# Where the top half of a float64 weight is merged: a second ScalarE pass into PSUM and one shift-or, for 36 of 64 tiles

## The chip, the cores and the metric

One Trainium2 chip, one core of it. The metric is device time of one execution in microseconds, as a median over several runs.

## The reference, cut to what matters

A block-wise linear attention (2 batches, 8 heads, 768 tokens, head size 64), a layer with a two-dimensional Fourier mix and a residual MLP (512 to 2048 to 512), and a second residual MLP layer with a scaled norm. The MLP weights come as float64:

```python
x = attn_out                        # (2, 768, 512)
u = x + real(fft(fft(x, axis=1), axis=2))
x = u + relu(norm(u) @ w_ch1) @ w_ch2           # layer one
x = x + relu((norm(x) * g_ln) @ w_ch1b) @ w_ch2b   # layer two
```

## The kernel before, in words

**Weights.** Each layer has 16 tiles of 128 x 512 of w1 (kind 1) and 16 of w2 (kind 2). A tile arrives as raw float64 words by a DMA into a `ws` buffer (`w_load`, L253), shifted by two bytes, so that 32 bits of each word hold the low part and one bfloat16 the high part. `conv_steps` (L285) makes float32 out of it, and then a float16 pair (hi, lo) for matmuls at half width. It is a generator of four steps:

1. ScalarE copies the high bfloat16, times two, to float16, into every other half-word of one of three `top` buffers (L294). The other half-words are zero from the start, so a `top` read as int32 has those 16 bits shifted up by 16.
2. VectorE shifts the low part right by 13 (L296) and ors the `top` into it (L297); the result is the float32 tile `wf` (tag `wt`, three buffers). Where the caller names a PSUM tag (`which`), the shifted part goes to a bank of that tag; otherwise it is made in place in SBUF.
3. ScalarE copies to float16 `hi` (L310); for layer two's w1 it first scales by the norm's gain (L309).
4. GpSimd makes `lo`, the remainder (L312).

**PSUM.** Eight banks in three tags: "at" three, "dn" three, "up" two (L141 to L144). `bank(which, name)` (L146) asks for a bank, and the tile framework assigns banks, adds the semaphore waits, and orders what is not ordered by hand, with a simulated time line. The fast MLP matmuls (`mlp_up_fast`, L789) take a `left` bank of "up" and a `right` bank of "at" for every pair of 128 hidden units. All automatic conversions use "at".

**The order at the start.** Attention of batch 0 runs task by task; its last chunk, the Fourier transform, the first norm and the first matmuls of layer one follow a hand-written order, the string ORDER (L44 to L49). For TensorE, VectorE, ScalarE and GpSimd it is binding (L962): each token is a piece of work, or the next step of a generator. The tokens around the change:

```
c0 S B1 B0 s s B1 B0 s s O4 B1 B0 O4 c0 I O4 R I O5 O5 O5 O5 c0 c1 c2 W12 k2 j2 k2 k2 d24 d20 d21 j2 j2 d22 d23
k1 k1 k1 d14 d10 d11 j1 j1 j1 d12 d13 c3 j0 j0 j0 d03 k0 k0 k0 d02 c1 D3 R c2 R c0 D2 d04 d01 D4 d00 c3 D1 q0 D0 q0
```

c0 to c3 are the conversions of layer one's first four w1 tiles (L949: c0 has the tag "at", c1 to c3 have none). S are the scores of chunk 5 (two "at" banks), I the inter-chunk product and O5 the output of chunk 5 (an "up" bank each). W12 is twelve matmuls on constant data into an "up" bank (L967 to L971) that nothing reads. k and j are the folds of batch 0 on VectorE (`fold_half`, L490); dmg are matmuls of the first transform (L522), Dg ScalarE's copies of its groups (L536), R the folding of one row, q and p the second transform (L584, L560). The third token of c1, its VectorE step, stands in the second line behind the last k0.

**Layer two's tiles.** Six w2 tiles are converted early and parked in DRAM (`w_stage`, L273, at steps 37 to 47 of 128 of the main loop); the others are converted from step 52 to 81 (`w1_unit`, L1046, and L1056). Layer one's tiles 4 to 15 of w1 and all of w2 are converted in the first 15 steps.

Of the kernel before, what the change touches and what calls it, by code (L numbers as in the profile page):

```python
# [9 lines left out]
F16 = mybir.dt.float16  # L10
BF16 = mybir.dt.bfloat16
F32 = mybir.dt.float32
I32 = mybir.dt.int32
I16 = mybir.dt.int16
AF = mybir.ActivationFunctionType
ALU = mybir.AluOpType
# [3 lines left out]
P = 128  # L20
# [20 lines left out]
TOPS = 2.0  # L41
# [83 lines left out]
def tile_retention_fourier_mlp(ctx: ExitStack, tc: tile.TileContext, a: dict, out: bass.AP):  # L125
    nc = tc.nc
    pe, act, dve, pool, sp = nc.tensor, nc.scalar, nc.vector, nc.gpsimd, nc.sync
# [18 lines left out]
    def bank(which, name):  # L146
        return banks[which].tile([P, 512], F32, tag=which, name=name)
# [105 lines left out]
    def w_load(kind, m, i, room=None):  # L253
        t = room
        if t is None:
            t = wst.tile([P, 512, 2], I32, tag="ws", name=f"ws{kind}_{m}_{i}")
        staged[kind, m, i] = t
        return sp.dma_start(t.rearrange("p n two -> p (n two)").bitcast(I16)[:, :2047], w_src(kind, m, i).bitcast(I16)[:, 1:2048])

    tops = [const.tile([P, 512, 2], F16, name=f"top{i}") for i in range(3)]  # L260
    for t in tops:
        pool.memset(t.rearrange("p n two -> p (n two)").bitcast(I32), 0)
    n_top = [0]

    def run(steps):
        for t in steps:
            pass
        return t

    def w_conv(kind, m, i):  # L270
        return run(conv_steps(kind, m, i, "at"))

    def w_stage(i):  # L273
        t = hl(f"wst2_{i}")
        run(conv_steps(2, 1, i, "at", t))
        away[i] = dram.tile([P, 2, 512], F16, name=f"wd{i}")
        sp.dma_start(away[i], t)
# [7 lines left out]
    def conv_steps(kind, m, i, which=None, into=None):  # L285
        if (kind, m, i) not in staged:
            w_load(kind, m, i)
        raw = staged.pop((kind, m, i))
        top = tops[n_top[0] % 3]
        n_top[0] += 1  # L290
        t = wtp.tile([P, 512], F32, tag="wt", name=f"wf{kind}_{m}_{i}")
        ti = t.bitcast(I32)
        part = ti if which is None else bank(which, f"ps_w{kind}_{m}_{i}").bitcast(I32)
        act.activation(top[:, :, 1], raw.bitcast(BF16)[:, :, 2], AF.Copy, scale=TOPS)  # L294
        yield t
        dve.tensor_scalar(part, raw[:, :, 0], 13, None, op0=ALU.logical_shift_right)  # L296
        dve.tensor_tensor(ti, part, top.rearrange("p n two -> p (n two)").bitcast(I32), op=ALU.bitwise_or)  # L297
        yield t
        if kind == 1:
            g, k = divmod(i, 4)  # L300
            if (m, g) not in w1t:
                w1t[m, g] = wpool.tile([P, 2, 4, 512], F16, tag=f"w1_{g}", name=f"w1_{m}_{g}")
            hi, lo = w1t[m, g][:, 0, k], w1t[m, g][:, 1, k]
        else:
            if into is None:
                into = w2t[m, i] = wpool.tile([P, 2, 512], F16, tag=f"w2_{i}", name=f"w2_{m}_{i}")
            hi, lo = into[:, 0], into[:, 1]
        if kind == 1 and m == 1:
            act.activation(t, t, AF.Copy, scale=gcol[:, k:k + 1])  # L309
        act.copy(hi, t)  # L310
        yield t
        (dve if m == 0 and i in (LD1 if kind == 1 else LD2) else pool).tensor_tensor(lo, t, hi, op=ALU.subtract)  # L312
        yield t
# [634 lines left out]
    for i in range(NE, 4):  # L948
        chains[f"c{i}"] = lambda i=i: conv_steps(1, 0, i, None if i else "at")  # L949
# [62 lines left out]
    for c in range(NCH):  # L1012
        t = B1 + SPC * c
# [3 lines left out]
    n = t + DC + DFO  # L1017
# [42 lines left out]
    def step(n):  # L1060
        m = n // (NB * NF)
        return m, order[m][n // NF % NB], n % NF
# [13 lines left out]
    for n in range(total + LAG):  # L1076
        rest = None
        if n < total:
            m, blk, f = step(n)
# [34 lines left out]
```

## Time and profile before

| | |
|---|---|
| median of 3 runs | 600.88 us (600.83 to 600.90) |
| the profiled execution | 601.57 us, span 599.8 us |
| TensorE matmul busy | 575.0 us, 96% of the span |
| VectorE busy | 412.2 us, 69% |
| ScalarE busy | 260.6 us, 43% |
| GpSimd busy | 278.5 us, 46% |

How to read it: times are microseconds unless marked ns, and positions are counted from the start of the span. PE is TensorE, PEld its weight loads, DVE VectorE, ACT ScalarE, POOL GpSimd, SP the engine that issues most DMAs. L12 is line 12 of the kernel. An arrow `out<-in` gives the tiles by name. "idle before <-X" is the time in which the engine had nothing to run, and what ended it; this is inferred from semaphores. Matmuls are pipelined, so single durations overlap. PEclk is the clock granted to TensorE as a share of full speed (1.00 is 2.4 GHz, 0.50 is 1.2 GHz).

### The profile page before, as it was taken

To read this page: it belongs to the slowest core of one execution; us is meant where nothing else is said; L and a number is where in the kernel's file an instruction comes from. 1 tells how busy PE (TensorE), PEld (TensorE's weight loads), DVE (VectorE), ACT (ScalarE), POOL (GpSimd) and SP (SyncE) were. 2 spreads that over 40 slices of the span, in tenths; PEclk is the share of its full clock that TensorE was granted. 3 is DMA by queue.
4 is the path that set the end of the run, shared out by engine and by line. 5 is a ranking of instruction groups with operands and counts; after the bars stand their busy time and mean duration, and the time that the engine had idled before them with its cause. 6 is when DMAs were issued, how large, how long until landed. Compare 5 with 4: busy or idle time off the path is not lost.

```text
span 599.8 us, 11798 instructions
## 1 busy us (share of the span) xinstructions
PE 575.0 (96%) x4629; PEld 378.2 (63%) x4629; DVE 412.2 (69%) x901; ACT 260.6 (43%) x525; POOL 278.5 (46%) x294
## 2 busy tenths in 40 slices
PE   7889999999999998999979999999999999999997
PEld 5746645566545554676747776666677777767773
DVE  6997899775893798877597679866535453555333
ACT  3646789663322433453557665743222322322110
POOL 8936889985443756442459765863011200110000
PEclk8999999999999999999998999999999999999999
DMA  8994269851000101352154543500110025002001
GB/s 283 411 412 164 88 210 342 264 187 37 1 1 1 36 19 22 102 153 94 37 194 146 170 143 101 145 19 2 62 27 19 2 83 60 19 1 85 22 2 52
DMA packets 46326, 63.23 MB, mean 105 GB/s; under 512 B 26176, under 2 KB 28350, under 8 KB 46270
## 3 DMA queue, kind: packets, MB, share of 16 engines
q1 hardware_dynamic: 45598, 62.40, 32.7%
q8 instruction: 36, 0.59, 0.4%
q10 hardware_dynamic: 672, 0.08, 0.1%
q14 instruction: 20, 0.16, 0.1%
HBM read 52.23 MB, written 6.29 MB: 98 GB/s over the span
## 4 chain that ended last, share of the span: by engine, by line
PE 62%; DVE 19%; POOL 7%; ACT 7%; issue 3%; DMA 1%; SPq 0%; DVEq 0%; POOLq 0%; ACTq 0%
PE ps_y L855 30%; PE ps L808 21%; PE ps_h L715 5%; POOL w L312 2%; DVE wf L297 2%; PE ps_s L350 2%; DVE bst L649 2%; DVE tr L768 2%; ACT top L294 1%; PE ps_d L525 1%; DVE ps_w L296 1%; POOL m L362 1%; ACT w L310 1%; ACT wf L309 1%; DVE h L841 1%
## 5 line engine op out<-in xcount | busy, mean ns | idle before, releaser
L855 PE MATMUL ps_y<-w,h 128*128 128x512 f16 x1152 | 282.1, 380 | 3.5 <-ACT h L840 1.7
L855 PEld LDWEIGHTS <-h 128*128 128x128 f16 x1152 | 109.3, 98 | 102.5 <-ACT h L840 3.8
L808 PEld LDWEIGHTS <-sw 128*128 128x128 f16 x1104 | 95.2, 98 | 23.3 <-issue 7.1
L808 PE MATMUL ps<-th,sw 128*128 128x192 f16 x828 | 93.2, 247 | 5.1 <-DVE s L821 3.6
L808 PEld LDWEIGHTS <-w 128*128 128x128 f16 x828 | 72.2, 98 | 19.1 <-issue 1.1
L312 POOL TENSOR_TENSOR w<-wf,w 128x512 f16<-128x512 f32 x58 | 67.3, 1166 | 36.0 <-ACT w L310 35.9
L840 ACT ACTIVATE h<-ps 128x384 f16<-128x384 f32 x92 | 43.7, 488 | 73.2 <-DVE ps L834 68.8
L715 PE MATMUL ps_h<-unT,w 128*128 128x384 f16 x396 | 73.7, 326 | 1.7 <-DVE h L730 1.6
L808 PE MATMUL ps<-unT,w 128*128 128x192 f16 x552 | 63.2, 247 | 0.0
L841 DVE SCALAR_TENSOR_TENSOR h<-ps,h 128x384 f16<-128x384 f32 x92 | 49.5, 554 | 13.2 <-ACT h L840 11.6
L715 PEld LDWEIGHTS <-w 128*128 128x128 f16 x396 | 37.0, 98 | 29.8 <-issue 3.1
L760 POOL TENSOR_TENSOR sw<-ws,sw 128x512 f16<-128x512 f32 x32 | 37.9, 1200 | 34.1 <-ACT sw L759 34.1
L828 DVE TENSOR_TENSOR t<-ps,s 128x192 f32<-128x192 f32 x46 | 16.3, 354 | 49.7 <-PE ps L808 49.4
L294 ACT ACTIVATE top<-ws 128x512 f16<-128x512 bf16 x57 | 44.3, 779 | 10.4 <-DVE wf L297 10.3
L820 ACT COPY s<-ps 128x192 f32<-128x192 f32 x46 | 14.5, 314 | 72.7 <-PE ps L808 72.7
L678 POOL TENSOR_TENSOR uns<-un,uns 128x512 f16<-128x512 f32 x21 | 24.6, 1173 | 43.8 <-ACT uns L677 43.7
L297 DVE TENSOR_TENSOR wf<-ps_w,top 128x512 int32<-128x512 int32 x61 | 41.3, 682 | 3.6 <-POOL w L312 2.3
L784 POOL TENSOR_TENSOR th<-ts,th 128x384 f16<-128x384 f32 x24 | 22.2, 943 | 42.8 <-ACT th L783 42.8
L310 ACT CAST w<-wf 128x512 f16<-128x512 f32 x58 | 34.9, 610 | 10.2 <-DVE wf L297 10.0
L296 DVE TENSOR_SCALAR ps_w<-ws 128x512 int32<-128x512 int32 x55 | 37.8, 689 | 0.9
L834 DVE TENSOR_TENSOR ps<-ps,s 128x192 f32<-128x192 f32 x46 | 16.7, 362 | 29.6 <-PE ps L808 29.5
L821 DVE TENSOR_TENSOR s<-ps,s 128x192 f32<-128x192 f32 x46 | 16.2, 352 | 28.0 <-ACT s L820 27.9
(163 smaller groups left out, 796.0 us busy)
## 6 DMA issues: line engine op xcount, KB each, us to landing
ws<-in_w SPq DMA_DIRECT2D x25, 511.8 KB, 4.5
ws<-in_w2b SPq DMA_DIRECT2D x16, 511.8 KB, 3.3
ws<-in_w1b SPq DMA_DIRECT2D x16, 511.8 KB, 4.3
kt<-in_kt SPq DMA_DIRECT2D x12, 256.0 KB, 3.6
qt<-in_qt SPq DMA_DIRECT2D x12, 256.0 KB, 5.5
v<-in_v SPq DMA_DIRECT2D x12, 256.0 KB
k<-in_k SPq DMA_DIRECT2D x12, 256.0 KB, 5.5
pre<-in_w SPq DMA_DIRECT2D x4, 511.8 KB
```

What stands on the lines that cost most here:

```text
L294: act.activation(top[:, :, 1], raw.bitcast(BF16)[:, :, 2], AF.Copy, scale=TOPS)
L296: dve.tensor_scalar(part, raw[:, :, 0], 13, None, op0=ALU.logical_shift_right)
L297: dve.tensor_tensor(ti, part, top.rearrange("p n two -> p (n two)").bitcast(I32), op=ALU.bitwise_or)
L310: act.copy(hi, t)
L312: (dve if m == 0 and i in (LD1 if kind == 1 else LD2) else pool).tensor_tensor(lo, t, hi, op=ALU.subtract)
L678: pool.tensor_tensor(s_[:, 1], un, s_[:, 0], op=ALU.subtract)
L715: pe.matmul(ps, w[:, i, k, fo:fo + P], x[:, j, k, :], start=n == 0, stop=n == 11)
L760: pool.tensor_tensor(lo, z, hi, op=ALU.subtract)
L808: pe.matmul(ps, lhs, rhs, start=start and n == 0, stop=n == 5, skip_group_check=True)
L840: act.activation(hi, z, AF.Relu)
L841: dve.scalar_tensor_tensor(lo, z, 0.0, hi, op0=ALU.max, op1=ALU.subtract)
L855: pe.matmul(dn[blk][j], h[:, x, j * P:(j + 1) * P], w[:, y], start=f == 0 and n == 0, stop=f == NF - 1 and n == 2)
```

## The change

For layer two's tiles (m = 1) and the first four w1 tiles of layer one, ScalarE makes the float16 of the high part into a plain buffer `half`, then reads its bits as bfloat16 and copies them, in a second pass, as float32 into a PSUM bank. A bfloat16 written as float32 has its bits in the upper half of the word, so this bank holds what `top` held. VectorE then shifts the low part and ors the bank in one `scalar_tensor_tensor`. The bank is "at" where the caller named it, and "up" for c1 to c3. All other tiles of layer one keep the old way and are alone in using the three `top` buffers.

```diff
+    halves = ctx.enter_context(tc.tile_pool(name="halves", bufs=2))
...
         raw = staged.pop((kind, m, i))
-        top = tops[n_top[0] % 3]
-        n_top[0] += 1
         t = wtp.tile([P, 512], F32, tag="wt", name=f"wf{kind}_{m}_{i}")
         ti = t.bitcast(I32)
-        part = ti if which is None else bank(which, f"ps_w{kind}_{m}_{i}").bitcast(I32)
-        act.activation(top[:, :, 1], raw.bitcast(BF16)[:, :, 2], AF.Copy, scale=TOPS)
-        yield t
-        dve.tensor_scalar(part, raw[:, :, 0], 13, None, op0=ALU.logical_shift_right)
-        dve.tensor_tensor(ti, part, top.rearrange("p n two -> p (n two)").bitcast(I32), op=ALU.bitwise_or)
-        yield t
+        high = raw.bitcast(BF16)[:, :, 2]
+        if m == 1 or (kind == 1 and i < 4):
+            half = halves.tile([P, 512], F16, tag="half", name=f"half{kind}_{m}_{i}")
+            part = bank(which or "up", f"ps_w{kind}_{m}_{i}")
+            act.activation(half, high, AF.Copy, scale=TOPS)
+            act.copy(part, half.bitcast(BF16))
+            yield t
+            dve.scalar_tensor_tensor(ti, raw[:, :, 0], 13, part.bitcast(I32), op0=ALU.logical_shift_right, op1=ALU.bitwise_or)
+            yield t
+        else:
+            top = tops[n_top[0] % 3]
+            n_top[0] += 1
+            part = ti if which is None else bank(which, f"ps_w{kind}_{m}_{i}").bitcast(I32)
+            act.activation(top[:, :, 1], high, AF.Copy, scale=TOPS)
+            yield t
+            dve.tensor_scalar(part, raw[:, :, 0], 13, None, op0=ALU.logical_shift_right)
+            dve.tensor_tensor(ti, part, top.rearrange("p n two -> p (n two)").bitcast(I32), op=ALU.bitwise_or)
+            yield t
```

## Rows read from the trace of the kernel before

**Rows 1.** The page: the span, and part 1, busy time of each engine.

```profile
span 599.8 us, 11798 instructions
...
PE 575.0 (96%) x4629; PEld 378.2 (63%) x4629; DVE 412.2 (69%) x901; ACT 260.6 (43%) x525; POOL 278.5 (46%) x294
```

**Rows 2.** Busy time by stretch: stretch, length, each engine (instructions), PEclk, DMA share, GB/s.

```profile
440.00:500.00 60.00, 60.00 (x486) 42.28 (x485) 29.02 (x75) 15.47 (x34) 8.12 (x9) 1.00 0.17 36
```

**Rows 3.** Timeline of PE, 33 to 50: start, length, instruction [idle before <-releaser].

```profile
33.30 0.86 PE L430 MATMUL ps_o<-vhl,m 128*128 128x64 f16 x24
34.24 1.47 PE L971 MATMUL warm<-expo 128*128 128x256 f16 x12
37.11 1.33 PE L522 MATMUL ps_d<-cs,f 128*1 128x385 f32 x3 [1.39 <-DVE f L502]
...
49.27 1.60 PE L584 MATMUL ps_pq<-cdsd,cst 128*128 128x128 f32 x12
```

**Rows 4.** Timeline of DVE, 43 to 45.

```profile
43.98 0.29 DVE L502 TENSOR_TENSOR f<-e 128x129 f32<-128x129 f32 x1
44.19 0.42 DVE L296 TENSOR_SCALAR wf<-ws 128x512 int32<-128x512 int32 x1
```

**Rows 5.** Timeline of ACT, 140 to 142.

```profile
140.51 0.78 ACT L294 ACTIVATE top<-ws 128x512 f16<-128x512 bf16 x1
```

**Rows 6.** Timeline of DVE, 186 to 300.

```profile
186.59 0.56 DVE L542 SCALAR_TENSOR_TENSOR cst<-ps_d,cst 128x385 f16<-128x385 f32 x1 [3.97 <-ACT cst L540]
...
237.00 0.68 DVE L296 TENSOR_SCALAR ps_w<-ws 128x512 int32<-128x512 int32 x1
...
290.93 0.69 DVE L863 SCALAR_TENSOR_TENSOR u<-ps_y,u 128x512 f32<-128x512 f32 x1 [1.61 <-PE ps_y L855]
293.65 0.36 DVE L828 TENSOR_TENSOR t<-ps,s 128x192 f32<-128x192 f32 x1 [2.02 <-PE ps L808]
...
298.38 0.54 DVE L841 SCALAR_TENSOR_TENSOR h<-ps,h 128x384 f16<-128x384 f32 x1
...
299.17 0.68 DVE L296 TENSOR_SCALAR ps_w<-ws 128x512 int32<-128x512 int32 x1
```

**Rows 7.** Groups by line and shape: instruction, count | busy us, mean ns | idle before.

```profile
L297 DVE TENSOR_TENSOR wf<-ps_w,top 128x512 int32<-128x512 int32 x61 | 41.3, 682 | 3.6 <-POOL w L312 2.3
L296 DVE TENSOR_SCALAR ps_w<-ws 128x512 int32<-128x512 int32 x55 | 37.8, 689 | 0.9
L310 ACT CAST w<-wf 128x512 f16<-128x512 f32 x58 | 34.9, 610 | 10.2 <-DVE wf L297 10.0
...
L357 DVE SCALAR_TENSOR_TENSOR m<-ps_s,mask 128x512 f32<-128x512 f32 x24 | 15.5, 680 | 2.1 <-PE ps_s L350 2.1
```

**Rows 8.** Busy time by stretch around two gaps of PE, columns as in rows 2.

```profile
233.90:240.00 6.10, 4.32 (x31) 2.66 (x30) 4.74 (x9) 2.71 (x6) 3.16 (x4) 1.00 0.29 54
310.00:314.90 4.90, 1.31 (x12) 1.01 (x12) 4.85 (x13) 3.39 (x8) 3.26 (x5) 1.00 0.36 110
316.00:320.00 4.00, 4.00 (x21) 2.63 (x19) 2.51 (x6) 1.43 (x4) 4.00 (x5) 0.57 0.20 45
```

**Rows 9.** Timeline of ACT, 36 to 50.

```profile
36.77 1.40 ACT L294 ACTIVATE top<-ws 128x512 f16<-128x512 bf16 x2
...
49.25 0.78 ACT L294 ACTIVATE top<-pre 128x512 f16<-128x512 bf16 x1
49.91 0.46 ACT L536 ACTIVATE cst<-ps_d 128x385 f32<-128x385 f32 x1
```

**Rows 10.** Timeline of DVE, 309 to 315.

```profile
309.64 0.68 DVE L296 TENSOR_SCALAR ps_w<-ws 128x512 int32<-128x512 int32 x1
...
314.51 0.34 DVE L821 TENSOR_TENSOR s<-ps,s 128x192 f32<-128x192 f32 x1
```

**Rows 11.** Timeline of PE, 314 to 386.

```profile
314.90 0.66 PE L808 MATMUL ps<-th,sw 128*128 128x192 f16 x6 [2.21 <-DVE s L821]
...
385.28 0.60 PE L855 MATMUL ps_y<-w,h 128*128 128x512 f16 x2 [0.72 <-ACT h L840]
```

## Prediction

> **What bounds the kernel now.** I read the page first, then the busy time by stretch, then the start engine by engine. The execution that the rows come from took 601.57 us, 0.7 above the median of 600.88; its span is 599.8, so 1.8 us lie around it. I add differences to the median. TensorE is busy for 575 of 599.8 us [rows 1], and late in the kernel it has no gap at all [rows 2]. So from the first full block on, time is TensorE's work plus its gaps, and whatever delays its start comes through one to one. There are two places where the changed code meets such a time. One is the written-out start: TensorE ends chunk 5's output matmuls at 34.16, runs the twelve warming matmuls W12 at 34.24, and does the first transform from 37.11 until the first sine matmul of the second transform (q0) at 49.27, almost without a break [rows 3]. VectorE makes the folds meanwhile; the last fold instruction starts at 43.98 and only then come c1's two merge instructions [rows 4]. The other is the middle of layer two's conversions.
>
> **The bank order decides.** In the changed code c1 and c2 take a bank of the two-bank tag "up" in their first step, by ScalarE's second pass, and give it back only when VectorE has merged. In ORDER these steps stand ahead of W12, which needs an "up" bank too, and c1's merge stands behind all folds. Does a bank go to whoever is ready first, or in the order in which the code was written? The trace of before has a test. Layer two's first conversions were loaded early: the third `top` pass for one of them ran at 140.51 [rows 5]. Its VectorE shift needs nothing else but a bank of "at". Yet VectorE idles 3.97 us before 186.59, when only the transform of group 0 holds such a bank, and the shift comes at 237.00, when the block with the `right` banks begins. The next one waits likewise: VectorE idles 1.61 us before 290.93 and 2.02 before 293.65, and the shift starts at 299.17, a quarter of a microsecond after the relu remainder at 298.38 has ended and freed an older `right` bank [rows 6]. A free bank is kept for tiles written earlier. So I take it that W12 comes third in line behind c1 and c2, and its bank is c1's.
>
> **Part by part.** (a) *W12 waits.* The last fold instruction ends at 43.98 + 0.29 = 44.27. The merge takes 0.68: VectorE's three-operand form with one PSUM source averages 680 ns (L357), the present or with a PSUM source 682 [rows 7]; no row has this form with integers, so its bounds are 0.66 and the two instructions of now, 0.69 + 0.68 = 1.37. W12 starts at 45.0 instead of 34.24. W12's own run is 1.47, then the transform from 37.11 to 49.27 takes its 12.16 with all folds ready: q0 at 58.65, **+9.4**. Behind W12 in TensorE's queue stand all transforms of the start; ScalarE's group copies, the second transform, the norm and the first layer's matmuls wait for them in turn. TensorE's old idle before 37.11 (1.39, for folds) is already taken out in this sum. (b) *The clock.* TensorE was idle for 3.6 of the 4.9 us before 314.9, and from 316 to 320 the granted clock was 0.57, near the lower of the two levels; 1.8 idle of the 6.1 us around 237 left it at 1.00 [rows 8]. Ten idle microseconds will lower it too: 4 us at 0.57 lose 4 x 0.43 = **+1.7**; bounds 0 and twice that. (c) *c0.* ScalarE works 0.5 to 0.6 us longer at 25.6, and a bank of "at" is taken before chunk 5's scores. It can cost 0 to 0.6, one cast [rows 7]; I take **+0.2**, as the attention's chain there runs over several engines in turn. VectorE's saved shift at 32 I cost at nothing: what follows waits for TensorE, which is at the last chunk's matmuls until 34.16 [rows 3]; without that cover it would be a gain of 0.7. (d) *ScalarE's prefetch.* The three `top` buffers are no longer used by c0 to c3, so the passes for the next three tiles can move ahead. The one at 49.25 stands before group 0's copy at 49.91 [rows 9]: **-0.4**, between 0 and its 0.65. (e) *c1 to c3's merges* save VectorE over 2 us after 44.2, worth nothing, for TensorE is the late one there, now more than before. (f) *Layer two.* Each of 32 tiles saves VectorE one instruction of 0.69. From 310 to 314.9 VectorE is busy 4.85 of 4.90 us, while TensorE waits 3.6 [rows 8], 2.21 of it for the addition at 314.51 [rows 10, 11]. Four of the shifts to be dropped stand ahead of that addition, the first at 299.17 and the last at 309.64: 4 x 0.69 = 2.8 off a gap of 3.6. What is left, 0.8, is below the 1.8 that did not lower the clock, so its 1.7 come back too: **-4.5**. Elsewhere TensorE has hardly a gap and the savings are hidden by its matmuls. (g) *ScalarE's extra passes in layer two.* No row shows ScalarE writing PSUM; the cast of the same size takes 0.61 [rows 7], the strided first pass 0.78 [rows 9]. I take 0.61. It counts where TensorE waits for ScalarE, as 0.72 us at 385.28 [rows 11]: none, or two passes late (1.2); I take one, **+0.6**. The loads and the queues of SP and GpSimd keep their instructions.
>
> The Trainium skill, ScalarE: Activation LUTs, section "Step-by-step: what each stage is for", says that ScalarE writes PSUM faster than SBUF, useful only where TensorE does not need most of PSUM. By its first half (g) would fall somewhat below 0.6; its caveat is the case here, since TensorE's W12 and the `right` banks want the same tags. No run here shows such a write yet.
>
> Sum: 0.2 + 9.4 + 1.7 - 0.4 - 4.5 + 0.6 = +7.0, **607.9 us**. With no loss of clock at the start and (c) and (g) at zero it is 9.4 - 0.4 - 4.5 = +4.5, 605.4; with nothing won in layer two, (c) and (g) at their upper ends and no prefetch gain, 0.6 + 9.4 + 1.7 + 1.2 = +12.9, 613.8. That is this case's own range.
>
> **Rivals.** *A. Banks go to whoever is ready.* Then W12 takes its bank at 34.24 as now, long before c1's second pass can come: its first pass starts at 36.77 [rows 9]. TensorE runs on as now. Only c3's second pass finds both banks held until c1's merge ends at 44.95, and holds ScalarE's queue, with the group copies behind it, for one pass longer, 0.6. The rest stays: 0.2 + 0.6 - 0.4 - 4.5 + 0.6 = -3.5, **597.4**, faster. It decides at one point: it holds if W12 starts at 34.3 and not at 45. For it: rows 6 show a bank unused, and a planner that wrongly thought VectorE busy would leave the same picture. Against it: twice the idle time was long, and the shift came within 0.3 us of a release. *B. Banks held in layer two.* The hold lies at the start as forecast, but "at" banks are then held from ScalarE's pass to the merge, with VectorE late, and the `right` banks of TensorE's next pair wait. At half of the 26 tiles that are not parked early, for 0.61 each, that is 13 x 0.61 = +7.9 on 607.9, about **616**. Against it: now too a bank is held from the shift to the or, and TensorE waits for VectorE's additions, not for banks, in its longest gap. *C.* The start's loss and the middle's gain cancel; this needs a hold of some 4 us only, and nothing in rows 4 would free c1's bank at 38.
>
> **Numbers.** Forecast case 0.72, A 0.19, B 0.06, C 0.03. Predicted 607.9. The 80% range reaches from 597, into A (whose own spread is about 595 to 600), to 614, the upper end of the forecast case; about 0.08 of A, 0.06 of B and 0.05 of the forecast lie outside. Two tenths of a per cent, 1.2 us, is what a measurement of this kernel can tell from no change. Faster by more: 0.18, nearly all of A; within: 0.04; slower: 0.78.
>
> **What would show it.** In the changed trace: W12 (L971) near 45, TensorE idle for over 10 us before it and waiting for VectorE's new merge line; the merge near 0.68 us, starting at about 44.3; the granted clock below 1.00 just after 45; q0 between 58 and 61; then a gap near 310 to 325 that is shorter than 3.6 us, relative to the blocks around it, with no fall of the clock. If W12 starts at 34.3 the step (a) is wrong and A holds. If the merge takes over 1 us, (f) is.

## The result and the profile after

The changed kernel takes 607.43 us (606.83 to 607.73, four runs) against 600.89: a ratio of 1.0107, 95% interval 1.009 to 1.0125, **6.5 us slower**. The forecast was 607.9, range 597 to 614. Its profiled execution took 606.83 us.

On the page of the changed kernel VectorE has lost 36 instructions and 18.8 us, ScalarE has gained 36 and 19.0 [rows 1]:

```profile
span 605.0 us, 11801 instructions
...
PE 571.4 (94%) x4629; PEld 375.6 (62%) x4629; DVE 393.4 (65%) x865; ACT 279.6 (46%) x561; POOL 279.0 (46%) x294
```

The start on TensorE, a timeline as in [rows 3] (past line 288 of the kernel before, line numbers are 11 higher in the changed one, so L971 is L982, L522 is L533, L584 is L595, L821 is L832, L855 is L866; in the kernels of the next section they move with each edit):

```profile
32.75 0.86 PE L441 MATMUL ps_o<-vhl,m 128*128 128x64 f16 x24
44.38 2.74 PE L982 MATMUL warm<-expo 128*128 128x256 f16 x12 [10.76 <-DVE wf L299]
47.05 2.94 PE L533 MATMUL ps_d<-cs,f 128*1 128x385 f32 x6
49.83 1.45 PE L533 MATMUL ps_d<-sn,f 128*128 128x384 f32 x4
...
59.85 1.60 PE L595 MATMUL ps_pq<-cdsd,cst 128*128 128x128 f32 x12
```

VectorE at the end of the folds, as in [rows 4]:

```profile
43.44 0.29 DVE L513 TENSOR_TENSOR f<-e 128x129 f32<-128x129 f32 x1
43.64 1.28 DVE L299 SCALAR_TENSOR_TENSOR wf<-ws,ps_w 128x512 int32<-128x512 int32 x2
```

ScalarE's second passes for c1 and c2:

```profile
37.40 0.59 ACT L297 CAST ps_w<-half 128x512 f32<-128x512 bf16 x1
...
38.62 0.59 ACT L297 CAST ps_w<-half 128x512 f32<-128x512 bf16 x1
```

TensorE is done with chunk 5 at 33.61, and then stands until W12 at 44.38. What it waits for is the new merge on L299, the first of the two that follow the last fold; the bank that it reads has been full since 37.99. Then W12 itself needs 2.74 instead of 1.47. The busy time by stretch (columns as in rows 2) has the clock, and the old gap near 310:

```profile
30.00:42.00 12.00, 2.15 (x43) 1.90 (x38) 10.47 (x26) 8.40 (x16) 3.94 (x6) 0.84 1.03 411
42.00:56.00 14.00, 11.62 (x36) 5.46 (x36) 2.85 (x7) 1.74 (x4) 0.00 (x0) 0.77 0.50 178
...
300.00:320.00 20.00, 19.36 (x157) 13.22 (x156) 15.14 (x34) 13.34 (x25) 8.53 (x9) 1.00 0.43 133
320.00:340.00 20.00, 18.38 (x148) 12.82 (x147) 15.05 (x34) 16.82 (x34) 17.24 (x18) 1.00 0.51 159
```

**Where the time went.** Two events cut every trace into three stretches: TensorE's first output matmul of layer one (`ps_y`), and the one wait of 1.61 us that both kernels have near the end of its slow matmuls (`ps_h`). These matmuls open the 36th of layer one's 64 steps; the fast ones (`mlp_up_fast`) begin right behind them. So the middle stretch is layer one up to this step, with batch 1's attention and transform in it. The rest of the span is the other 29 steps of layer one and all of layer two, and the merges of all of layer two's tiles lie there. In the kernel before:

```profile
67.36 0.59 PE L855 MATMUL ps_y<-w,h 128*128 128x512 f16 x2
...
235.72 2.11 PE L715 MATMUL ps_h<-unT,w 128*128 128x384 f16 x12 [1.61 <-DVE h L730]
```

In the changed one:

```profile
77.71 0.59 PE L866 MATMUL ps_y<-w,h 128*128 128x512 f16 x2
...
247.83 2.11 PE L726 MATMUL ps_h<-unT,w 128*128 128x384 f16 x12 [1.61 <-DVE h L741]
```

The start grew by 10.35 us, the middle by 1.76 (170.12 against 168.36), the rest of the span shrank by 6.91 (357.17 against 364.08): 5.2 between the spans. The medians lie 6.5 apart: the profiled execution of before took 0.7 more than its median (its granted clock up to 30 us was 0.94, against 1.00 in the one of after), that of after 0.6 less than its own.

The same three stretches in the profiled execution of every kernel tried (all named in the next section):

| kernel | start | middle | rest of span | median us |
|---|---|---|---|---|
| before | 67.36 | 168.36 | 364.08 | 600.9 to 601.2 |
| changed | 77.71 | 170.12 | 357.17 | 607.43 |
| first four tiles only | 77.46 | 168.33 | 363.81 | 612.21 |
| layer two only | 66.81 | 169.81 | 357.28 | 597.45 |
| W12 ahead of c1, c2 | 67.29 | 170.51 | 357.30 | 596.90 |
| c1, c2 without a bank | 66.73 | 169.88 | 357.29 | 596.12 |
| c1's merge early | 72.13 | 169.79 | 357.38 | 600.98 |
| no W12 | 68.48 | 168.83 | 357.29 | 596.37 |
| layer two, no banks | 66.93 | 169.16 | 363.91 | 602.63 |
| layer two, second pass twice | 66.86 | 170.29 | 364.85 | 603.69 |
| before + pass into PSUM | 66.87 | 168.42 | 369.81 | 606.68 |
| before + pass into SBUF | 67.00 | 168.41 | 364.19 | 601.11 |
| w1 tiles of layer two only | 66.84 | 168.45 | 366.91 | 604.79 |
| every tile, c1, c2 without a bank | 67.21 | 165.06 | 357.23 | 591.55 |

(In layer two without banks the wait at the cut is 0.70 instead of 1.61, and eight of the fast matmuls and three merges of layer two stand ahead of it and twelve more slow matmuls behind it, so its middle and rest compare with the others only to within one or two microseconds.)

Past the second cut the tile framework orders the instructions by itself, anew for every kernel. Instruction by instruction, the order on TensorE, VectorE and ScalarE there is the same in the seven kernels of 357.2 to 357.4, and the same in the two of 363.8 and 364.1. Each of the other five has an order of its own, so their times hold the new order as well as the edit.

### The profile page after: what moved, and what is told of

It reads as the page before. It is cut to its first block, busy times and chain, and to the rows that moved or that the text cites. A ratio compares the mean times of both kernels' runs of the same rounds, so it can differ in the third digit from the quotient of the medians.

```text
span 605.0 us, 11801 instructions
## 1 busy us (share of the span) xinstructions
PE 571.4 (94%) x4629; PEld 375.6 (62%) x4629; DVE 393.4 (65%) x865; ACT 279.6 (46%) x561; POOL 279.0 (46%) x294
## 5 line engine op out<-in xcount | busy, mean ns | idle before, releaser
L866 PE MATMUL ps_y<-w,h 128*128 128x512 f16 x1152 | 279.4, 379 | 3.4 <-ACT h L851 1.5
L866 PEld LDWEIGHTS <-h 128*128 128x128 f16 x1152 | 109.3, 98 | 104.5 <-ACT h L851 3.8
L668 POOL TENSOR_TENSOR rs<-rs,neghalf 128x1 f32<-128x1 f32 x24 | 13.1, 548 | 48.1 <-DVE rs L666 47.6
L299 DVE SCALAR_TENSOR_TENSOR wf<-ws,ps_w 128x512 int32<-128x512 int32 x35 | 23.8, 683 | 15.1 <-ACT ps_w L297 8.3
L832 DVE TENSOR_TENSOR s<-ps,s 128x192 f32<-128x192 f32 x46 | 16.2, 353 | 25.8 <-ACT s L831 25.7
L373 POOL TENSOR_TENSOR m<-m,m 128x512 f16<-128x512 f32 x24 | 30.7, 1294 | 1.5 <-ACT m L371 1.5
```

What stands on the lines that cost most here:

```text
L299: dve.scalar_tensor_tensor(ti, raw[:, :, 0], 13, part.bitcast(I32), op0=ALU.logical_shift_right, op1=ALU.bitwise_or)
L373: pool.tensor_tensor(t[:, 1], m32, t[:, 0], op=ALU.subtract)
L866: pe.matmul(dn[blk][j], h[:, x, j * P:(j + 1) * P], w[:, y], start=f == 0 and n == 0, stop=f == NF - 1 and n == 2)
```

## The experiments

### The start alone, layer two alone

The start alone:

```
-        if m == 1 or (kind == 1 and i < 4):
+        if m == 0 and kind == 1 and i < 4:
```

> Only the first four tiles of layer one take the new way; layer two keeps its two VectorE instructions. Hold theory (c1 and c2 own the two up banks, W12 waits for c1's merge): q0 near 59.9 as in the changed kernel (10.6 later than before), nothing comes back later, and the gap of 3.6 us near 310 is there again, some 10.6 later: 611 to 612 us. Rival (the start is partly made up later, layer two gives nothing): the same 607.4 as the changed kernel.

Measured: 612.21 us, ratio 1.0186 (1.0171 to 1.0202). The waits of TensorE (tile and line, releaser, total, times, longest) hold both the new one and the old gap near 310 [rows 11]:

```profile
PE warm L982 <- DVE wf L299: 10.8, 1, 10.8
PE ps L819 <- DVE s L832: 3.6, 2, 2.2
```

Layer two alone:

```
-        if m == 1 or (kind == 1 and i < 4):
+        if m == 1:
```

> Only layer two's tiles take the new way; c0 to c3 keep the old one. Hold theory: W12 at 34.2 as before, the gap of 3.6 us at 310 to 314.9 and its fall of the clock are gone: 600.9 - 4.0 = 596.9, in 596 to 598, faster than both kernels. Rival (the later 4 us came only because the late start moved conversions against TensorE's work): no change, 600.9. Rival B (banks of at held in layer two cost time): over 601.

Measured: 597.45 us, ratio 0.9948 (0.9932 to 0.9965); the profiled execution is the fastest of four (595.64 to 598.68). W12 starts at 33.71. So the two parts are separate: one costs 11.2, the other gives 3.5, and their sum is the changed kernel's +6.5 to within 1.2 us. But the gap near 310 is not gone. TensorE is idle for 2.26 us between 300 and 320, at a clock of 1.00, and the cause is new. TensorE there:

```profile
312.77 0.66 PE L819 MATMUL ps<-th,sw 128*128 128x192 f16 x6 [1.32 <-DVE wf L299]
```

VectorE's merge:

```profile
312.04 0.68 DVE L299 SCALAR_TENSOR_TENSOR wf<-ws,ps_w 128x512 int32<-128x512 int32 x1
```

ScalarE's second pass for the same tile:

```profile
307.14 0.59 ACT L297 CAST ps_w<-half 128x512 f32<-128x512 bf16 x1 [0.74 <-DVE h L852]
```

ScalarE took a bank at 307.14, VectorE merged at 312.04, and TensorE stood for that bank. In the kernel before, a bank was held from the shift at 309.64 [rows 10] to the or at 311.31. ScalarE in turn waits for banks in its second pass (waits of ScalarE):

```profile
ACT ps_w L297 <- DVE h L852: 9.0, 11, 1.5
```

The middle is 1.45 longer, though no tile of layer one was changed. ScalarE's first pass for a layer-two tile that is parked early stands ahead of the chunk's `vhl` pass and waits for its weights:

```profile
122.51 0.66 ACT L296 ACTIVATE half<-ws 128x512 f16<-128x512 bf16 x1 [2.40 <-DMA ws<-in_w2b]
...
125.25 0.62 ACT L339 ACTIVATE vhl<-v 128x512 f16<-128x512 f32 x1
```

TensorE is late a little after:

```profile
130.09 0.48 PE L361 MATMUL ps_s<-qt,kt 64*128 64x128 f32 x2 [1.07 <-DVE u L447]
```

A wait of ScalarE for these weights, 1.4 to 3.1 us, is in every kernel of the table whose middle takes 168.8 to 170.5, the 1.4 in the one of 168.83; in none of those with 168.3 to 168.5. No run takes this wait away alone, so it goes with the loss and is not shown to be its cause.

### Is it the bank, and its order?

Four kernels, each the whole change with one edit. W12 ahead of c1 and c2 in ORDER:

```
-c0 c1 c2 W12 k2 j2
+c0 W12 c1 c2 k2 j2
```

> The whole change, but W12 stands ahead of c1 and c2 in ORDER. Hold theory (banks go out in written order): W12 takes its bank first, starts near 34.3 and the start runs as before; with layer two's gain about 597. Rival (ScalarE's extra passes at the start cost the time, not the bank): W12 early, but q0 still several us later than 49.3 and over 601 in all.

Measured: 596.90 us, ratio 0.9935 (0.992 to 0.995). TensorE:

```profile
33.84 1.47 PE L982 MATMUL warm<-expo 128*128 128x256 f16 x12
...
49.44 1.60 PE L595 MATMUL ps_pq<-cdsd,cst 128*128 128x128 f32 x12
```

ScalarE, c3's second pass:

```profile
44.55 0.59 ACT L297 CAST ps_w<-half 128x512 f32<-128x512 bf16 x1 [3.90 <-DVE wf L299]
```

c1 and c2 without a bank:

```
-            part = bank(which or "up", f"ps_w{kind}_{m}_{i}")
+            part = t if which is None and i < 3 else bank(which or "up", f"ps_w{kind}_{m}_{i}")
```

> The whole change in its written order, but c1's and c2's second ScalarE pass writes their own SBUF tile in place of an up bank, and the merge reads it there. Hold theory (the bank alone holds W12): W12 near 34.3, q0 near 49.5, about 597 to 598. Rival (the order of the steps, not the bank): W12 at 44.4 as in the changed kernel, 607. The first four second passes also show what the write costs into SBUF against PSUM: 0.61 against 0.58 if the cast to SBUF is a measure.

Measured: 596.12 us, ratio 0.9925 (0.99 to 0.9951). TensorE:

```profile
32.90 0.86 PE L441 MATMUL ps_o<-vhl,m 128*128 128x64 f16 x24
33.84 1.47 PE L982 MATMUL warm<-expo 128*128 128x256 f16 x12
...
48.87 1.60 PE L595 MATMUL ps_pq<-cdsd,cst 128*128 128x128 f32 x12
```

c1's merge early:

```
-d22 d23
+d22 d23 c1
...
-d02 c1 D3 R c2 R
+d02 D3 R c2 R
```

> The whole change, but c1's merge stands on VectorE after the first third of the folds instead of behind all of them. Hold theory: c1's second pass ends at 38.0, the merge follows, W12 starts at 38.7 to 38.9 rather than 44.4, the transform's 12.2 us from there put q0 at 52.5 to 54, and the time lies between 600 and 602. Rival (TensorE waits for the last folds, the bank only goes with them): q0 near 60, 607.

Measured: 600.98 us, ratio 0.9997 (0.9987 to 1.0007). TensorE:

```profile
38.86 2.74 PE L982 MATMUL warm<-expo 128*128 128x256 f16 x12 [5.15 <-DVE wf L299]
...
54.29 1.60 PE L595 MATMUL ps_pq<-cdsd,cst 128*128 128x128 f32 x12
```

No W12, which leaves out twelve matmuls whose result nothing reads:

```
-c0 c1 c2 W12 k2 j2
+c0 c1 c2 k2 j2
```

> The whole change without the twelve warming matmuls W12 (their result is not used). Hold theory (W12 alone wants the bank, the transforms behind it do not): the first transform matmul at 36.7 as in the kernel before, q0 at 49 to 50, 597; up to 1.9 more, the clock's loss of the changed kernel, if three idle microseconds lower the granted clock too: 597 to 599. Rival (the transforms or ScalarE are held by c1's and c2's banks as well): q0 near 59, 607.

Measured: 596.37 us, ratio 0.9925 (0.9907 to 0.9944). TensorE:

```profile
36.78 3.02 PE L533 MATMUL ps_d<-cs,f 128*1 128x385 f32 x6 [2.95 <-DVE f L513]
39.59 2.46 PE L533 MATMUL ps_d<-sn,f 128*128 128x384 f32 x4
...
50.63 1.60 PE L595 MATMUL ps_pq<-cdsd,cst 128*128 128x128 f32 x12
```

With the same work on every engine, moving one word of ORDER ahead of two others brings W12 from 44.38 to 33.84. With the words where they were but the two passes into SBUF, it is the same 33.84. So it is the bank, and the written order decides who gets it. W12 follows c1's merge wherever that is put: 38.86 for a merge after a third of the folds. Without W12 the transforms wait only for folds; their q0 comes later than the 49 to 50 expected, at 50.63, and so does that of the early merge, 54.29 for 52.5 to 54, by what the lower clock costs (below). In the first of the four, c3's pass finds both banks held by c1 and c2, and ScalarE stands 3.90 us with the group copies behind it: q0 is 0.57 later than with no banks.

### What layer two pays with, and what for

The kernel before, with one extra pass in layer two into the bank that VectorE's shift then overwrites:

```
         act.activation(top[:, :, 1], raw.bitcast(BF16)[:, :, 2], AF.Copy, scale=TOPS)
+        if m == 1:
+            act.copy(part.bitcast(F32), top.rearrange("p n two -> p (n two)").bitcast(BF16)[:, :512])
```

> The kernel before, with VectorE's two instructions kept everywhere, and in layer two one extra ScalarE pass of 512 columns into the tile's at bank ahead of the shift (the shift writes over it). It prices the change's cost in layer two without its saving, the early hold of the bank with it. Step (g) as predicted: one pass late, 0.6 above the kernel before, 601.5 (601 to 602.2). Rival (a pass costs as in the run with the second pass doubled, 6.2 for 32 of them): 605 to 609, and then what VectorE's saving is worth by itself is 8 to 12 us, not 4.5.

The same, with `spare`, an SBUF tile that nothing reads, in place of the bank:

> As the run with the extra pass into the bank, but the extra pass writes an SBUF tile that nothing reads, so no bank is held for it. If ScalarE's time alone is what costs: the same time as that run, within 1 us. If the bank held from ScalarE's pass on is what costs: near the kernel before, 601 to 602, and below that run.

The extra pass into the bank takes 606.68 us (ratio 1.0087, 1.0073 to 1.01), the same pass into SBUF 601.11 (0.999, 0.9979 to 1.0001). So 32 more passes on ScalarE cost the kernel before nothing measurable, and writing them into the bank costs 5.6 us; step (g) had 601 to 602.2 for it. More than one thing comes with the bank. It is held from the pass on, ScalarE has to wait for a free one, and VectorE's shift, which overwrites it, has to wait for the pass. The group of the shifts, into the bank:

```profile
L298 DVE TENSOR_SCALAR ps_w<-ws 128x512 int32<-128x512 int32 x55 | 37.9, 691 | 15.9 <-ACT ps_w L296 15.0
```

The same group with the pass into SBUF:

```profile
L300 DVE TENSOR_SCALAR ps_w<-ws 128x512 int32<-128x512 int32 x55 | 37.8, 689 | 0.8
```

The two kernels also differ in the framework's order. The pair gives the price of all this together, and no run separates the hold from the waits or from the order. With the bank, TensorE's longest wait past the cut is for an activation of ScalarE, which itself waited for an addition of VectorE and not for a bank:

```profile
315.24 1.03 PE L857 MATMUL ps_y<-w,h 128*128 128x512 f16 x2 [3.99 <-ACT h L842]
```

ScalarE's extra pass (L296) waits nine times for a bank, seven for a relu remainder (L843) and two for an or (L299) to let go:

```profile
ACT ps_w L296 <- DVE h L843: 5.2, 7, 0.9
...
ACT ps_w L296 <- DVE wf L299: 1.8, 2, 1.1
```

Layer two alone, with the second pass made twice:

```
             act.copy(part, half.bitcast(BF16))
+            if m == 1:
+                act.copy(part, half.bitcast(BF16))
```

> Layer two alone takes the new way, and its second ScalarE pass is made twice: 32 more passes of 0.59 us. Theory (ScalarE has room, a pass counts only where TensorE waits for it, one or two times): 0 to 1.2 above layer two alone, 597.4 to 598.6. Rival (ScalarE's passes set the time of layer two): a large part of 32 x 0.59 = 18.9 us, over 603.

Measured: 603.69 us (ratio 1.004, 1.0025 to 1.0055), 6.2 above layer two alone, against 0 to 1.2 expected. Here too the bank is held for longer, and the wait near 316 is long again (L821 and L834 are L808 and L821 of the kernel before):

```profile
316.37 0.66 PE L821 MATMUL ps<-th,sw 128*128 128x192 f16 x6 [3.37 <-DVE s L834]
```

Layer two alone, with no banks:

```
-            part = bank(which or "up", f"ps_w{kind}_{m}_{i}")
+            part = t
```

> Layer two alone takes the new way, and its second ScalarE pass writes the SBUF tile instead of an at bank. Theory (in the run with layer two alone TensorE's last wait near 312, 1.32 us for a merge at 312.04, is for the bank that ScalarE took at 307.14): that wait goes, the gap between 300 and 340 shrinks from 2.5 to about 1.2 us, and the time is some 1.3 below that run's, near 596. Rival (VectorE's additions are as late without it): the same wait under another name, no change, 597.4. Prices: write into SBUF 0.62 as for two passes of the earlier run, against 0.59; merge from two SBUF sources 0.69, or 1.0 and more beside GpSimd, as SBUF operations of VectorE at 300.15 and 307.30 show.

Measured: 602.63 us (ratio 1.0027, 1.0017 to 1.0038), no way out. The bank wait of 1.3 is gone, but the merge from two SBUF tiles takes 1038 ns on average instead of 683. Its group of L299 (line, tiles, shapes, count | busy, mean ns | idle before):

```profile
L299 DVE SCALAR_TENSOR_TENSOR wf<-ws,wf 128x512 int32<-128x512 int32 x32 | 33.1, 1038 | 16.7 <-ACT wf L297 12.4 <-POOL ws L767 4.0
```

Two of its merges on VectorE:

```profile
319.07 1.02 DVE L299 SCALAR_TENSOR_TENSOR wf<-ws,wf 128x512 int32<-128x512 int32 x1 [0.86 <-ACT wf L297]
...
342.56 0.69 DVE L299 SCALAR_TENSOR_TENSOR wf<-ws,wf 128x512 int32<-128x512 int32 x1
```

The group in layer two alone:

```profile
L299 DVE SCALAR_TENSOR_TENSOR wf<-ws,ps_w 128x512 int32<-128x512 int32 x32 | 21.9, 683 | 15.1 <-ACT ps_w L297 8.3 <-POOL w L323 2.9 <-POOL ws L765 1.9
```

GpSimd is idle from 341.85 to 343.13, around the one of 0.69, and busy through the one of 1.02. All 20 merges of over 0.9 us began while a GpSimd instruction ran; of the 12 shorter ones, ten began with GpSimd idle and two in the last 0.2 us of an instruction. The Trainium skill, SBUF — State Buffer, section "SBUF: two separate sides", says that a VectorE operation with two SBUF inputs and a GpSimd operation that reads SBUF lock each other out for a whole instruction; the rows go with that. This run also closes what stood against the written order: its first conversions of layer two ran long before the `right` banks were in use, now that they need none, at 140.72 against 237.00 for the first shift in the kernel before [rows 6]:

```profile
140.72 1.81 DVE L299 SCALAR_TENSOR_TENSOR wf<-ws,wf 128x512 int32<-128x512 int32 x2
```

### Half of layer two, and every tile

Only the w1 tiles of layer two:

```
-        if m == 1 or (kind == 1 and i < 4):
+        if m == 1 and kind == 1:
```

> Only the 16 first-matrix tiles of layer two take the new way. Theory by shares (VectorE's time taken off ahead of the two gaps near 310 and 424 counts): about half of layer two's gain, 599 (598 to 600). Rival (the fall of the clock alone decides, and any relief that brings the first gap below 3 us gives it back): nearly all of it, 597.5. Rival (the second-matrix tiles are the ones in the way): 601.

Measured: 604.79 us, ratio 1.006 (1.004 to 1.0081): half the change is slower than none or all of it. TensorE's waits for activations and additions have grown, and ScalarE again waits for banks (4.9 us in six waits for the relu remainder). None of the three theories held. Why the mixture is worse than either way alone is open; the order past the cut is its own here too.

Every tile, with c1 and c2 without a bank as above:

```
-        if m == 1 or (kind == 1 and i < 4):
+        if True:
```

> Every tile takes the new way, c1 and c2 without a bank. Beside the earlier run with c1 and c2 without a bank (596.1), VectorE loses 28 more instructions of 0.69, all in layer one, and ScalarE gets 28 passes of 0.59. Theory (layer one's savings are hidden: TensorE waits there for VectorE only 2.7 us in all, and those waits are not behind conversions): no change by over 1 us, 595 to 597.5. Rival (a pass on ScalarE, or its wait for a bank, delays the group copies and activations of layer one): 600 or more.

Measured: 591.55 us, ratio 0.9837 (0.9824 to 0.9851). **It beats both kernels**, the kernel before by 9.7 us. The rest of the span is the 357.2 of the others; the middle is 4.8 shorter than with the old way for layer one's tiles, 165.06 against 169.88. ScalarE does not wait for the parked tiles' weights there, which goes with 1.45 above (its one wait for weights, 0.4 us, is for a tile of layer one). Another 0.8 is TensorE's wait for the first full block's weights. With c1 and c2 alone without a bank:

```profile
77.73 0.81 PE L866 MATMUL ps_y<-w,h 128*128 128x512 f16 x3 [1.08 <-ACT w L321]
```

With every tile in the new way:

```profile
76.59 0.81 PE L866 MATMUL ps_y<-w,h 128*128 128x512 f16 x3 [0.30 <-ACT w L321]
```

Of the remaining 2.6, some 0.8 lie ahead of these two matmuls and the rest between them and 155, where TensorE shows as busy nearly throughout in both traces; what makes them up was not settled. The expectation, that layer one's savings are hidden, was wrong.

## Why the prediction was right

**The bank order** was right and is now shown by three edits: who is written first, whether a bank is needed at all, and when the first holder lets go. Rival A (banks to whoever is ready) falls with them. Its own side term was right, though: where W12 goes first, c3's pass holds ScalarE until c1's merge, and q0 loses 0.57 (0.6 in the rival).

**(a)** W12 was to wait from 34.24 to 45.0. It waits until 44.38, but chunk 5 ended 0.55 earlier too (33.61 for 34.16), so the hold is 10.69 against 10.76 predicted. The merge takes 0.64 to 0.69 (0.68 taken).

**(b)** The clock cost W12 1.27 (2.74 for 1.47) and the first transforms 0.65 (from L533's first row to its second, 2.78 against the 2.13 from 36.57 to 38.70 in layer two alone): 1.9 for 1.7. Ten idle microseconds were not needed for it: five lowered it as much (c1's merge early), and three without W12 cost 1.7, with q0 16.8 after the end of chunk 5's matmuls there (33.83) against 15.1 in the kernel before.

**(c)** c0: chunk 5 starts its output matmuls at 32.90 in the two runs above that show it, between 32.63 and 32.97 in all seven with c0 in the new way, and at 32.76 in layer two alone: 0.2 at most, either way, for 0.2. **(d)** From there to the first `ps_y` it is 33.83 with the passes moved ahead (no banks for c1, c2) and 34.05 without (layer two alone): -0.22 for -0.4. **(e)** nothing, as said. The four terms of the start sum to +10.9, of which (c) lies ahead of chunk 5; measured from chunk 5 on, the first `ps_y` moves from 34.06 to 44.96 us after it, by 10.9.

**(f) and (g)** are where the sum was right by luck: two errors cancel. The forecast was -4.5 + 0.6 = -3.9. Measured against the kernel before, the rest of the span is 6.9 shorter, and the middle 1.45 (1.76 in the changed kernel) longer: -5.2 by the profiled runs, and -3.5, -4.1 and -4.9 by the medians of the three kernels that keep the start. Step by step:
- The gap near 310 shrank by 1.44 (16.30 busy of 300 to 320 before, 17.74 in layer two alone), not 2.8, for the most part since the wait for the bank, 1.32, took the place of the additions' lateness. The clock came back as said: 0.91 of that stretch before is 0.09 x 20 = 1.8. The stretch before:

```profile
300.00:320.00 20.00, 16.30 (x117) 11.04 (x116) 17.88 (x37) 11.54 (x23) 12.58 (x14) 0.91 0.48 154
```

  In layer two alone:

```profile
300.00:320.00 20.00, 17.74 (x140) 12.00 (x139) 17.16 (x35) 16.04 (x33) 14.31 (x16) 1.00 0.49 157
```

- "Elsewhere TensorE has hardly a gap and the savings are hidden by its matmuls" was wrong. Between 400 and 440 the kernel before has a second gap, 2.4 us by the busy time of its stretches; in layer two alone it is closed (39.95 of 40 busy), which gave 2.3. With the two of the stretch at 310 that is 5.5 of the 6.9; the rest was not traced. The second gap before:

```profile
400.00:420.00 20.00, 19.00 (x146) 12.62 (x145) 12.55 (x31) 5.48 (x13) 5.89 (x6) 1.00 0.03 8
420.00:440.00 20.00, 18.63 (x163) 13.88 (x162) 10.90 (x27) 4.79 (x10) 1.67 (x2) 1.00 0.16 53
```

  Its longest wait is for the same addition as at 310:

```profile
423.85 0.66 PE L808 MATMUL ps<-th,sw 128*128 128x192 f16 x6 [1.37 <-DVE s L821]
```

- (g) priced ScalarE's time, which costs nothing measurable, and not the bank with the waits and the order that come with it, 5.6 in the one pair that shows it. Rival B had the hold and named a price of that size, 7.9, but put it on top of the forecast and on TensorE. In layer two alone TensorE waits for such a bank once, 1.32 us, and ScalarE eleven times, 9.0 us.
- VectorE's saving looks undersold as well. If the parts add, the rest of the span goes from 369.8, with the banks held early and both VectorE instructions kept, to 357.2: 12.6 for the 32 instructions dropped, less 5.7 for the banks (369.8 against 364.1). That is an estimate from three kernels with three orders; no run has the saving without the hold at the same merge time.
- Not in the sum at all: "The loads and the queues of SP and GpSimd keep their instructions" was meant to cost nothing, and yet ScalarE's queue in the middle stretch came to wait for one of them. The sum had priced a pass by its length, not by what it waits for.

The Trainium skill's page that the prediction weighed (ScalarE: Activation LUTs, section "Step-by-step: what each stage is for") is borne out in its first half. The pass takes 0.589 us into PSUM and 0.618 into SBUF (medians in the run with c1 and c2 without a bank, min/median/max):

```profile
L297 ACT CAST ps_w<-half x34: 571/589/610, 25.3 to 405.2; 128x512 f32<-128x512 bf16 x34
L297 ACT CAST wf<-half x2: 618/618/619, 37.6 to 38.8; 128x512 f32<-128x512 bf16 x2
```

Its caveat, that this is useful only where TensorE does not need most of PSUM, is borne out in part. The pass into banks that TensorE uses too cost the kernel before 5.6 us, but with the whole of layer two in the new way PSUM (597.45) still beats SBUF (602.63), where the merge has two SBUF sources.

## What to carry to other kernels

A step that moves to another engine is priced by what it holds and what it waits for, more than by its length: here 0.6 us passes were free into SBUF, and with an early bank and what waits for it they cost 5.6 us in one place and 10.8 in another. Where a framework orders the instructions, compare the orders of two kernels before a small difference is put down to the edit. Where buffers of a tag go out in written order, look for who is written first and released last; moving one word made the change faster than the kernel before. And when a sum comes out right, check its terms in stretches: (f) and (g) were both off by several microseconds, as far as the estimate above goes.

## What the runs showed that was not expected

- TensorE's clock fell after five idle microseconds as after eleven (W12 2.74 both times; 0.77 granted from 42 to 56 in the changed kernel, between its two levels of 0.50, 1.2 GHz, and 1.00, 2.4 GHz), and after three idle microseconds, with W12 left out, the first transforms took 3.02 + 2.46 for 2.30 + 1.45. The 1.7 us thus lost at q0 was partly made up: 168.83 in the middle stretch instead of 169.88.
- One VectorE instruction on integers from an SBUF and a PSUM source took 0.65 to 0.71 us in every run; from two SBUF sources 0.66 to 2.59.
- The four kernels of 596 to 597.5 us spread over 1.5 to 3.9 us in their four runs each, where 19 runs of the kernel before lie within 1.8. Their profiled executions all have 357.3 in the rest of the span; what the longer runs lose, and where, was not traced.
